# A kernel of cross attention and a two-layer perceptron with its order table, PSUM banks and SBUF rooms laid out anew

## The chip, the cores and the metric

The kernel runs on one core of a Trainium2 chip. The metric is device time in microseconds (us) of one execution. The engines are PE (matrix multiplication, with PEld for its weight loads), DVE (vector), ACT (scalar), POOL (GpSimd) and SP (which here issues transfers). Each works through its own queue in order; semaphores join them.

## The reference

For each of 8 batches and 8 heads, 512 tokens of 64 values and 32 states of 64 values attend to each other in both directions. The result, 544 rows of 512 values per batch, then goes through two layers with a leaky rectifier (alpha per column) between them.

```python
scores = scale * np.matmul(x, state.transpose(0, 1, 3, 2))
a = np.exp(scores - scores.max(-1, keepdims=True))
a /= a.sum(-1, keepdims=True) + 1e-09
xread = np.matmul(a, state)
scores2 = scale * np.matmul(state, x.transpose(0, 1, 3, 2))
...
sread = np.matmul(a2, x)
attn_out = np.concatenate([xread, sread], axis=2)
...
h = x @ w_in
g = np.maximum(h, 0.0) + alpha * np.minimum(h, 0.0)
return (g @ w_out).astype(np.float32)
```

## The kernel before

The work goes by batch. For the tokens of a batch, the states are first multiplied by w_in (m, step `m`, eviction `mo`), and the attention weights of the tokens (aT) then multiply m, so that h comes out at once, without xread. Sixteen tiles h of 128 columns of w_in by 512 tokens are made per batch (step `F`, L568). ACT makes neg = relu(-h) (step `N`, L621), DVE makes g = neg * (1 - alpha) + h (step `G`, L624). The state rows of all batches are gathered in XS and go through the layers as a ninth batch (L577, and steps of number 8).

The second layer of batch 0 is plain: 4 x 16 matmuls of 512 columns (step `S`, L638). For the other batches it is done in seven products of halves instead of eight: sums and differences of quarters of g (gsum, step `U`, L705) and of w_out (ws, step `W`, L681), products in three accumulators px, py, pv (step `P`, L726), copies of intermediate px (kept, step `K`, L742), and output quarters (oq, step `Q`, L759), stored by SP.

The weights of a batch come from scores (sc, L316), a transpose of 32x32 blocks on DVE (ts, L348), a maximum (mx, L381), a shift by it (step `ssh`, L386, mostly POOL), an exponential on ACT (L395), a sum and its reciprocal (r, L402 and L403), a normalisation (an, step `snorm`, L406), and a transpose back (aT, L414). Batch 0 is done in two halves j with PE transposes (tsc, L355; aT from at_ps, L370). The states' own reads of the tokens (sread) go through nb (L426), e (L443), a transposing transfer (e2T) and sr_ps (L469). A fill (step `Z`, L230) is a matmul of a constant pattern whose result is not used; `fill(0, 9)` puts nine of them at PE's start.

What stands where in the queues is not computed: the string ORDER lists some 1,100 steps, each a letter code with its batch, tile, engine (a, v, p for ACT, DVE, POOL) and PSUM bank, and the last loop of the function calls them in turn. Each step puts its instructions at the end of its engines' queues. Eight PSUM banks are six of one tag each (k0 to k5) and a pair with the tag `two`; SBUF tiles have tags by kind, with fixed numbers of buffers (three for xg, four for neg, two per g group).

Of the kernel before, what the change touches and what calls it, by code (L numbers as in the profile page):

```python
# [17 lines left out]
stc.0.a stt.0.1 sbd.0.a cx.0.0.v lst xt.0.0.0.2 cx.1.0.v sbd.1.a xt.0.1.0.3 xo.0.0.0.a tsc.0.0.4 xo.0.1.0.v tsc.1.0  # L18
cx.1.1.v Z.5.1 smax.0.0 xt.0.1.1.0 xo.0.1.1.v cx.0.1.a xt.0.0.1.2 ssh.v.0.0 sto.0.a Z.3.1 tsc.1.1.5 xo.0.0.1.a tsc.0.1
m.0.0.1.3 sexp.0.0 mo.0.0.a.1 Z.0.1 smax.0.1 ssh.v.0.1 sexp.0.1 wi.1 str.0.2 wi.2 sro.0.a ssum.0.0 lx.1 snorm.p.0.0  # L20
str.1.4 wi.3 sro.1.a ssum.0.1 oma Z.0.1 snorm.v.0.1 wo.1 Z.3.1 Z.5.1 m.0.1.0.3 mo.0.1.a.0 at.0.5 mo.0.1.a.1 at.1.2
ao.0.v wo.0 ao.1.v mo.0.0.a.0 m.1.0 mo.1.0.v F.0.7.4 N.0.7 G.0.7 F.0.6.0 F.0.2.5 N.0.6 F.0.1.3 G.0.6 N.0.2 m.2.2.2.1
N.0.1 mo.2.2.v.0 G.0.1 m.1.1 mo.1.1.a F.0.5.4 G.0.2 F.0.4.0 N.0.4 Z.2.1 N.0.5 m.0.2 mo.0.2.a F.0.3.2 F.0.0.3 N.0.0
G.0.4 G.0.5 Z.5.1 xt.1.1.1.0 xo.1.1.1.v G.0.0 N.0.3 G.0.3 F.0.8.5 N.0.8 xt.1.0.1.4 xo.1.0.1.a wo.2 lx.2 F.0.9.0 N.0.9
m.0.3 xt.1.1.0.3 G.0.8 xo.1.1.0.v xt.1.0.0.4 xo.1.0.0.v mo.0.3.a mo.2.2.a.1 Z.2.1 m.3.3.2.5 mo.3.3.a.0 sc.1 m.2.0.3.4
mo.2.0.a.0 mo.2.0.a.1 G.0.9 wo.3 mo.3.3.a.1 F.0.11.1 S.0.1.3.0 sb.1 smax.1 ssh.p.1 S.0.2.3.2 m.2.3.3.4 mo.2.3.a.0
N.0.11 W.1.0.p F.0.10.5 S.0.1.2 tm.1 S.0.2.2 G.0.11 N.0.10 G.0.10 F.0.12.3 W.1.1.p mo.2.3.a.1 S.0.1.0 F.0.14.4 N.0.12
G.0.12 nb.1.a sexp.1 F.0.15.1 ssum.1.5 te.1.1 te.1.0 F.0.13.3 N.0.13 tsum.1 S.0.2.1 snorm.v.1 S.0.1.5 S.0.1.4 N.0.15
m.1.3 mo.1.3.a S.0.1.1 wb.1 G.0.15 S.0.2.5 N.0.14 G.0.14 S.0.2.4 m.1.2 mo.1.2.a G.0.13 S.0.2.0 F.1.1.5 N.1.1 F.1.13.1
G.1.1 N.1.13 G.1.13 F.1.7.4 S.0.2.7 N.1.7 G.1.7 F.1.6.3 N.1.6 S.0.1.7 G.1.6 xd.2 F.1.10.5 N.1.10 G.1.10 F.1.12.1  # L30
S.0.2.6 N.1.12 G.1.12 tt.1 F.1.15.4 O.0.2.a N.1.15 G.1.15 F.1.14.3 N.1.14 G.1.14 W.2.0.p W.4.0.p S.0.1.6 O.0.1.a
S.0.3.7.5 m.6.3.2.1 sc.2 sb.2 mo.6.3.a.1 mo.6.3.a.0 S.0.0.7.4 lx.3 F.1.9.0 N.1.9 W.2.1.p S.0.3.6 F.1.0.3 N.1.0 F.1.5.1
N.1.5 tm.2 smax.2 S.0.0.2 G.1.5 W.3.1.p nb.2.a te.2.1 S.0.3.0 G.1.9 F.1.4.2 S.0.0.3 S.0.3.4 N.1.4 G.1.4 S.0.0.5 G.1.0
te.2.0 tt.2 tsum.2 F.1.11.1 N.1.11 G.1.11 W.4.1.p ssh.p.2 sexp.2 m.3.2 F.1.3.0 N.1.3 ssum.2.2 S.0.0.1 xd.3 S.0.3.2
S.0.3.5 mo.3.2.a S.0.0.4 S.0.3.1 S.0.3.3 F.1.8.3 O.0.3.a N.1.8 F.1.2.1 rd.1.5 G.1.3 rdo.1.1.a rdo.1.0.a snorm.v.2
rd.2.0 rdo.2.1.a m.2.1 G.1.8 rdo.2.0.a N.1.2 G.1.2 mo.2.1.a wb.2 P.1.1.0.1.5 S.0.0.0 S.0.0.6 O.0.0.a P.1.2.0.0.2
U.1.1.1.p sc.3 sb.3 P.1.1.1.0 tm.3 P.1.1.1.1 P.1.1.0.0 K.1.1.a F.2.8.0 F.2.0.3 N.2.8 G.2.8 smax.3 F.2.4.1 F.2.6.4
N.2.0 nb.3.a P.1.2.1.0 N.2.4 U.1.3.1.p N.2.6 G.2.6 P.1.2.0.1 U.1.2.1.p P.1.6.1.1 G.2.0 te.3.1 P.1.2.1.1 G.2.4 te.3.0
tt.3 tsum.3 lx.4 F.2.2.0 N.2.2 xd.4 U.1.1.0.p U.1.2.0.p P.1.6.0.0 P.1.6.1.0 P.1.6.0.1 Q.1.0.0 U.1.4.0.p K.1.2.a
ssh.p.3 F.2.12.4 F.2.15.3 N.2.12 G.2.2 F.2.13.1 G.2.12 N.2.15 G.2.15 F.2.11.2 N.2.11 G.2.11 N.2.13 F.2.5.0 N.2.5  # L40
G.2.13 G.2.5 P.1.5.0.1 P.1.5.1.1 P.1.5.1.0 sexp.3 ssum.3.4 P.1.5.0.0 K.1.4.a rd.3.3 rdo.3.0.a rdo.3.1.a m.3.0.2.1
# [769 lines left out]
```

## Time and profile before

| | |
|---|---|
| median of 3 runs | 209.4 us (209.06 to 209.43) |
| span of the profiled execution, first to last instruction | 207.2 us |
| instructions | 5043 |
| PE busy | 198.9 us, 2003 matmuls |
| DVE busy | 182.6 us |
| ACT busy | 148.7 us |
| POOL busy | 144.0 us |
| granted TensorE clock | 1.00 |

The profiled execution has no time of its own beside its span; the runs' median lies 2.2 us above it. Busy time is the time in which an engine has an instruction under way. A row of the timeline gives start, duration, engine, line, operation, out<-in and how many were merged; a row of groups gives busy us, the mean ns of one, and the idle time just before them with what ended it.

### The profile page before, as it was taken

What the parts mean: (1) busy time and instruction counts of PE and PEld (TensorE: products, weight loads), DVE (VectorE), ACT (ScalarE), POOL (GpSimd) and SP (SyncE); (2) the same over time, 40 slices, a digit from 0 to 9 for tenths busy, and PEclk for the clock granted to TensorE, in tenths of its full rate; (3) what the DMA queues carried; (4) which work ended last, traced back from release to release, by engine and by line L of the source; (5) the groups of instructions that cost most, each with busy time, mean ns of one, the idle gap of its engine ahead of it and who ended that gap; (6) DMA issues with size and microseconds to landing.
All of it is one profiled execution on the core that took longest, in us unless ns stands there. A gap on an engine that the chain in (4) does not pass through costs nothing.

```text
span 207.2 us, 5043 instructions
## 1 busy us (share of the span) xinstructions
PE 198.9 (96%) x2003; PEld 131.7 (64%) x2003; DVE 182.6 (88%) x277; ACT 148.7 (72%) x298; POOL 144.0 (70%) x87
## 2 busy tenths in 40 slices
PE   7789989999999999999999999999999999999992
PEld 2443433445666666677677766778767767888881
DVE  0899999999999999999999999998899988577650
ACT  3799998988789969988786899586677575321211
POOL 8173099999999999999897999949900697210100
PEclk9999999999999999999999999999999999999999
DMA  5999999949599999267979702112002021012134
GB/s 178 223 204 204 206 202 184 116 126 198 92 155 166 175 221 179 38 79 135 252 97 131 214 17 51 55 54 103 0 0 99 6 101 54 0 51 74 48 136 152
DMA packets 45943, 24.74 MB, mean 119 GB/s; under 512 B 24288, under 2 KB 45408, under 8 KB 45920
## 3 DMA queue, kind: packets, MB, share of 16 engines
q1 hardware_dynamic: 32960, 15.74, 31.2%
q0 software_dynamic: 12688, 8.62, 29.2%
q8 instruction: 15, 0.25, 0.5%
q10 hardware_dynamic: 272, 0.07, 0.1%
q14 instruction: 8, 0.07, 0.1%
HBM read 18.36 MB, written 8.91 MB: 132 GB/s over the span
## 4 chain that ended last, share of the span: by engine, by line
PE 81%; DVE 14%; issue 1%; DMA 1%; ACT 1%; POOL 0%; DVEq 0%; POOLq 0%; ACTq 0%
PE px L726 23%; PE h L568 23%; PE pv L726 12%; DVE g L624 7%; PE py L726 6%; PE o L638 6%; PE h L577 3%; PE m_ps L519 3%; PE fill L230 2%; DVE mx L381 1%; PE sr_ps L469 1%; DVE r L402 1%; DMA out_dram<-oq 1%; PE sc L316 1%; DVE ts L386 1%
## 5 line engine op out<-in xcount | busy, mean ns | idle before, releaser
L624 DVE SCALAR_TENSOR_TENSOR g<-neg,oma_sb,h 128x512 f16<-128x512 f32 (+1 forms) x144 | 94.5, 710 | 4.3 <-ACT neg L621 3.5
L621 ACT ACTIVATE neg<-h 128x512 f32<-128x512 f32 (+1 forms) x144 | 76.1, 590 | 14.0 <-PE h L568 8.2
L568 PE MATMUL h<-aT,m 128*128 128x512 f16 x256 | 64.5, 379 | 0.7 <-DVE g L624 0.5
L726 PEld LDWEIGHTS <-gsum 128*128 128x128 f16 x480 | 46.6, 98 | 9.6 <-issue 1.0
L568 PEld LDWEIGHTS <-m 128*128 128x128 f16 x256 | 24.1, 98 | 25.1 <-issue 4.3
L726 PEld LDWEIGHTS <-g 128*128 128x128 f16 x360 | 34.9, 98 | 7.3 <-issue 0.9
L705 POOL TENSOR_TENSOR gsum<-g 128x1024 f16<-128x1024 f16 (+1 forms) x14 | 28.7, 2060 | 14.4 <-PE pv L726 14.3
L705 POOL TENSOR_TENSOR gsum<-g,g 128x1024 f16<-128x1024 f16 x11 | 23.4, 2129 | 13.2 <-DVE g L624 13.1
L726 PE MATMUL px<-ws,gsum 128*128 128x256 f16 x240 | 29.8, 273 | 0.0
L742 ACT COPY kept<-px 128x512 f32<-128x512 f32 (+1 forms) x21 | 12.2, 582 | 23.8 <-PE px L726 22.8
L705 POOL TENSOR_TENSOR gsum<-gsum,g 128x1024 f16<-128x1024 f16 x11 | 23.4, 2126 | 3.4 <-DVE gsum L705 2.7
L705 POOL TENSOR_TENSOR gsum<-g,gsum 128x1024 f16<-128x1024 f16 x11 | 23.4, 2131 | 0.3
L545 ACT CAST m<-m_ps 128x512 f16<-128x512 f32 x36 | 19.9, 622 | 2.8 <-PE m_ps L519 2.7
L386 POOL TENSOR_TENSOR ts<-ts,mx 128x1024 f32<-128x1024 f32 x7 | 13.4, 1916 | 9.3 <-DVE mx L381 8.8
L638 PE MATMUL o<-w_out_sb,g 128*128 128x512 f16 x64 | 16.5, 379 | 0.0
L759 DVE TENSOR_TENSOR oq<-pv,kept 128x512 f32<-128x512 f32 (+1 forms) x16 | 10.5, 653 | 6.7 <-ACT kept L742 4.4
L726 PE MATMUL px<-w_out_sb,g 128*128 128x256 f16 x120 | 16.1, 273 | 0.0
L726 PE MATMUL px<-w_out_sb,gsum 128*128 128x256 f16 x120 | 16.1, 273 | 0.0
L726 PE MATMUL py<-w_out_sb,g 128*128 128x256 f16 x120 | 16.1, 273 | 0.0
L726 PE MATMUL pv<-ws,gsum 128*128 128x256 f16 x120 | 15.7, 273 | 0.0
L726 PE MATMUL pv<-ws,g 128*128 128x256 f16 x120 | 15.6, 273 | 0.0
L543 ACT CAST m<-m_ps 128x1024 f16<-128x1024 f32 x12 | 12.5, 1042 | 1.7 <-PE m_ps L519 1.6
(81 smaller groups left out, 232.7 us busy)
## 6 DMA issues: line engine op xcount, KB each, us to landing
out_dram<-oq SPq DMA_DIRECT2D x28, 256.0 KB, 2.6
xg<-in_x_dram POOLq DMA_DIRECT2D x8, 512.0 KB, 7.4
w_in_sb<-in_moe_w_in_dram POOLq DMA_DIRECT2D x4, 512.0 KB, 8.7
w_out_sb<-in_moe_w_out_dram POOLq DMA_DIRECT2D x4, 512.0 KB, 12.7
x<-in_x_dram SPq DMA_DIRECT2D x2, 512.0 KB, 4.9
out_dram<-osb SPq DMA_DIRECT2D x4, 256.0 KB, 4.3
out_dram<-oq SPq DMA_DIRECT2D x4, 128.0 KB, 2.1
st<-in_state_dram POOLq DMA_DIRECT2D x1, 224.0 KB, 7.3
```

What stands on the lines that cost most here:

```text
L386: engine(e).tensor_tensor(blocks(cols(live["ts", b], j, S)), blocks(scored(b, j)), over_blocks(cols(live["mx", b], j, S // N)), ALU.subtract,)
L519: nc.tensor.matmul(t[N * k : N * (k + 1), :], st_head(b, h)[64 * r : 64 * r + 64, :], w_in_sb[64 * r : 64 * r + 64, c, 512 * f : 512 * (f ...
L543: copier(e)(m_tile(b, f), t)
L545: copier(e)(m_tile(b, f)[:, g, :], t[g])
L568: nc.tensor.matmul(h.rearrange("p (r j s) -> p r j s", r=2, j=2), ms[b, f][:, g, 128 * j : 128 * (j + 1)], weights(b, g), start=(g == 0), ...
L621: nc.scalar.activation(neg, h, RELU, bias=0.0, scale=-1.0)
L624: nc.vector.scalar_tensor_tensor(g_tile(b, jc), negs.pop((b, jc)), oma_sb[:, jc : jc + 1], hs.pop((b, jc)), ALU.mult, ALU.add,)
L638: nc.tensor.matmul(outs[b, q], g_tile(b, jc)[:, 128 * q : 128 * (q + 1)], w_out_sb[:, jc, :], start=not begun and jc == 2 * jc2, stop=left ...
L705: engine(e).tensor_tensor(t, x(), y(), op)
L726: nc.tensor.matmul(pbanks[b, name][:, i, :], of(b, c)[:, j, 128 * i : 128 * (i + 1)], moving[:, 4 * c + j, :], start=not begun and j == 0, ...
L742: copier(e)(t, pbanks[b, "x"])
L759: nc.vector.tensor_tensor(osb, pbanks[b, name], kept[b, add], ALU.add)
```

## The change

All eight PSUM banks become one tile `banks`, and each step names the bank (or the first of two neighbours) that it uses; m, which used the pair or two banks, always uses two free banks and is evicted in two copies. The SBUF tiles that were in tags by kind come from two pools of equal rooms, small ones of 2 KB and large ones of 4 KB per partition; the number behind an @ in ORDER is the room, and a tile that takes a room waits until the last reader of the one before is done. The sum r of the tokens' weights lies in SBUF where the step says `s`; the normalisations on POOL read it there. The loads are issued in another order. ORDER is another list: the same kinds of steps (the same 2003 matmuls, 19 of them fills, six of which move from between the first steps to PE's start behind the nine), in another sequence, on engines partly changed.

```diff
-stc.0.a stt.0.1 sbd.0.a cx.0.0.v lst xt.0.0.0.2 cx.1.0.v sbd.1.a xt.0.1.0.3 xo.0.0.0.a tsc.0.0.4 xo.0.1.0.v tsc.1.0
-cx.1.1.v Z.5.1 smax.0.0 xt.0.1.1.0 xo.0.1.1.v cx.0.1.a xt.0.0.1.2 ssh.v.0.0 sto.0.a Z.3.1 tsc.1.1.5 xo.0.0.1.a tsc.0.1
...
+Z.1.1 Z.2.1 lst cx.0.0.v Z.3.1 Z.4.1 Z.7.1 Z.0.1 wi.1 stc.0.a cx.1.0.a stt.0.5 sbd.0.v sbd.1.v xt.0.0.0.6 xt.0.1.0.1
+xo.0.1.0.v@3 lx.1@4 xo.0.0.0.a cx.0.1.v tsc.0.0.4 tsc.1.0 smax.0.0 xt.0.0.1.3 cx.1.1.a xt.0.1.1.7 xo.0.1.1.v tsc.1.1.2
...
     att = ctx.enter_context(tc.tile_pool(name="att", bufs=2))
-    moe = ctx.enter_context(tc.tile_pool(name="moe", bufs=2))
+    rooms = ctx.enter_context(tc.tile_pool(name="rooms", bufs=1))
...
+    banks = ps.tile([128, 8, 512], F32, name="banks", bufs=1)
...
     def single(k, name, shape, dtype):
-        return ps.tile(shape, dtype, name=name, tag=f"k{k}", bufs=1)
-
-    def two(name, shape, dtype):
-        return ps.tile(shape, dtype, name=name, tag="two", bufs=1)
+        t = banks[:, k, :]
+        return shaped(t.bitcast(F16) if dtype == F16 else t, shape)
+
+    def two(k, name, shape, dtype):
+        return shaped(banks[:, k : k + 2, :].rearrange("p k c -> p (k c)"), shape)
...
+    place = [None]
+
+    def placed(name, shape, dtype):
+        n = 4 if dtype == F32 else 2
+        for d in shape[1:]:
+            n *= d
+        assert n <= 4096
+        tag = f"{'small' if n <= 2048 else 'large'}{place[0]}"
+        room = [shape[0], (2048 if n <= 2048 else 4096) // (4 if dtype == F32 else 2)]
+        return shaped(rooms.tile(room, dtype, name=name, tag=tag, bufs=1), shape)
...
-        xg = xgs[b] = att.tile([128, H, 2, 2, D], F16, name=f"xg_{b}", tag="xg", bufs=3)
+        xg = xgs[b] = placed(f"xg_{b}", [128, H, 2, 2, D], F16)
...
-        if b:
-            live["r1", b] = single(jk, f"r1_{b}", [128, 2 * S // N], F32)
-        r1 = cols(live["r1", b], j, S // N)
+        if b and jk != "s":
+            live["r1", b] = single(jk, f"r1p_{b}", [128, 2 * S // N], F32)
+        r1 = cols(soft_tile(b, "r1"), j, S // N)
...
-    def state_w_in(b, f, k0=None, k1=None):
-        if k0 is None:
-            live["mp", b, f] = two(f"m_ps{b}_{f}", [128, 2, 512], F32)
...
+    def state_w_in(b, f, k0, k1):
+        live["mp", b, f] = k0, k1
+        for g, k in enumerate((k0, k1)):
+            m_matmuls(single(k, f"m_ps{b}_{f}_{g}", [128, 512], F32), b, f, g)
+
+    def state_w_in_out(b, f, e, g):
+        copier(e)(m_tile(b, f)[:, g, :], banks[:, live["mp", b, f][g], :])
...
     for token in (globals().get("TOKENS") or ORDER).split():
+        token, _, where = token.partition("@")
+        place[0] = where
         name, *args = token.split(".")
```

ORDER's other lines are all replaced too. Its effect is shown at three places; names carry buffer numbers of the build.

The first is DVE's start, up to the second shift of batch 0. Before:

```order
L175 CAST xg_first<-x_0_70 128x4x128 x2
L306 COPY xT_first<-xT_psfirst_0_125 128x4x128
L175 CAST xg_first<-x_1_72 128x4x128
L381 TENSOR_REDUCE mx_146<-tsc_132 128x16
L306 COPY xT_first<-xT_psfirst_1_151 128x4x128
L386 TENSOR_TENSOR ts_145<-tsc_132,mx_146 128x512
L381 TENSOR_REDUCE mx_146<-tsc_167 128x16
L386 TENSOR_TENSOR ts_145<-tsc_167,mx_146 128x512
```

And in the change (`banks` is any PSUM bank; L302 copies the states into st_pairs, L215 casts x, L346 copies transposed x):

```order
L215 CAST xg_first<-x_0_71 128x4x128
L302 COPY st_pairs<-banks 64x8x32 x2
L346 COPY xT_first<-banks 128x4x128
L215 CAST xg_first<-x_1_73 128x4x128
L421 TENSOR_REDUCE mx_148<-banks 128x16
L346 COPY xT_first<-banks 128x4x128
L426 TENSOR_TENSOR ts_170<-banks,mx_148 128x512
L421 TENSOR_REDUCE mx_148<-banks 128x16
L426 TENSOR_TENSOR ts_170<-banks,mx_148 128x512
```

The copies into st_pairs have come to DVE, ahead of its first copy of transposed x; the cast of the first half of x has gone to ACT in part.

The second is ACT, from the first exponential of batch 0 to the first neg. Before:

```order
L395 ACTIVATE ts_145<-ts_145 128x512
L545 CAST m_0_188<-m_ps_0_1_178 128x512
L395 ACTIVATE ts_145<-ts_145 128x512
L281 COPY stT<-st_ps_196 128x128x7
L281 COPY stT<-st_ps_218 128x128x7
L545 CAST m_1_258<-m_ps_1_0_248 128x512
L545 CAST m_1_258<-m_ps_1_1_249 128x512
L545 CAST m_0_188<-m_ps_0_0_177 128x512
L621 ACTIVATE neg_7_289<-h_7_286 128x512
```

And in the change (L435 exponential, L571 eviction of m, L321 states, L411 weights aT, L610 neg):

```order
L435 ACTIVATE ts_170<-ts_170 128x512
L571 CAST m_0_181<-banks 128x512
L435 ACTIVATE ts_170<-ts_170 128x512
L571 CAST m_0_181<-banks 128x512
L321 COPY stT<-banks 128x128x7 x2
L411 COPY aT_233<-banks 128x512
L571 CAST m_1_249<-banks 128x512
L571 CAST m_0_266<-banks 128x512
L610 ACTIVATE neg_3_270<-banks 128x512
```

The first half of aT has come to ACT, behind the two copies of the states, and both halves of m for batch 0 are evicted ahead of it; DVE makes the other half of aT.

The third is POOL in the middle, where batches 3 and 4 are normalised. Before:

```order
L386 TENSOR_TENSOR ts_939<-ts_939,mx_940 128x1024
L158 DMA xg_1159<-in_x_dram 128x8x256
L705 TENSOR_TENSOR gsum_4_1_1179<-g_3_607,gsum_2_1_996 128x1024
L158 DMA xg_1195<-in_x_dram 128x8x256
L705 TENSOR_TENSOR gsum_3_0_1212<-g_0_603 128x1024
L681 TENSOR_TENSOR ws_736<-w_out_sb 128x1024
L705 TENSOR_TENSOR gsum_1_1_1274<-g_1_990,g_3_1061 128x1024
```

And in the change (L426 shift, L446 normalisation, L692 sums of g, L196 load of x):

```order
L426 TENSOR_TENSOR ts_912<-ts_912,mx_941 128x1024
L692 TENSOR_TENSOR gsum_4_1_1016<-g_3_574,gsum_2_1_727 128x1024
L692 TENSOR_TENSOR gsum_4_0_1048<-g_2_723,gsum_2_0_901 128x1024
L692 TENSOR_TENSOR gsum_3_1_1082<-g_1_586 128x1024
L446 TENSOR_TENSOR an_1094<-ts_912,r_3_1012 128x1024
L692 TENSOR_TENSOR gsum_3_0_1101<-g_0_927 128x1024
L692 TENSOR_TENSOR gsum_1_1_1103<-g_1_957,g_3_950 128x1024
```

The normalisation an of the batch stands on POOL, between sums of g; before it was DVE's, in this stretch `L406 TENSOR_TENSOR an_941<-ts_939,r_3_1094 128x1024`.

300 lines of the change are left out of this document (136 added, 164 removed).

## The prediction

> **What bounds the kernel now.** I read the page's busy shares and its chain first, then a table by stage.
>
> ```profile
> PE 198.9 (96%) x2003; PEld 131.7 (64%) x2003; DVE 182.6 (88%) x277; ACT 148.7 (72%) x298; POOL 144.0 (70%) x87
> ...
> PE 81%; DVE 14%; issue 1%; DMA 1%; ACT 1%; POOL 0%; DVEq 0%; POOLq 0%; ACTq 0%
> ```
>
> PE is busy for 198.9 of 207.2 us and carries 81% of the chain that ended last. An average over stages hides where the other 8.3 us lie, so here are five stages (us of the stage, then busy us and instructions of PE, PEld, DVE, ACT, POOL):
>
> ```profile
> 0.00:5.20 5.20, 3.75 (x9) 1.19 (x9) 0.39 (x3) 1.58 (x2) 4.49 (x12) 1.00 0.55 179
> 5.20:15.50 10.30, 8.24 (x109) 4.41 (x109) 9.39 (x20) 8.47 (x16) 4.24 (x6) 1.00 1.25 213
> 15.50:40.00 24.50, 23.44 (x208) 9.64 (x206) 24.39 (x37) 23.63 (x44) 15.64 (x11) 1.00 1.22 183
> 40.00:140.00 100.00, 99.92 (x1187) 66.04 (x1164) 98.47 (x139) 84.74 (x178) 93.49 (x49) 1.00 0.69 129
> 140.00:201.00 61.00, 61.00 (x499) 48.53 (x497) 48.52 (x81) 29.32 (x59) 26.14 (x13) 1.00 0.16 57
> ```
>
> From 40 to 201 us PE is without a matmul for 0.08 us. Nothing that the change does to other engines there can make it faster; it can only keep PE as full. Up to 40 us DVE and ACT are the full ones: from 15.5 to 40 DVE rests 0.11 us and ACT 0.87, and PE 1.06. From 40 to 140 DVE still rests only 1.5 of 100 us. So the time is: the moment at which the DVE and ACT work of batch 0 gets going, plus a PE stream that must not break. The end is short:
>
> ```profile
> 202.27 1.04 PE L726 MATMUL px<-w_out_sb,gsum 128*128 128x256 f16 x8
> ...
> 203.40 0.37 ACT L757 COPY oq<-px 128x256 f32<-128x256 f32 x1 [1.22 <-PE px L726]
> ```
>
> The last useful matmul ends at 203.3, and 3.9 us of eviction and store follow. The change ends in the same way (a quarter of the state rows, from DVE instead of ACT), so I leave this tail as it is. The median of the three runs is 209.4, the span of the profiled execution 207.2; the 2.2 us around it are carried over.
>
> **The start, step by step.** These rows of the timeline (start, us, engine, operation) are the path to the first h and the first g:
>
> ```profile
> 1.45 4.02 PE L230 MATMUL fill<-pattern 128*128 128x512 f16 x9 [1.45 <-POOL pattern L210]
> ...
> 4.88 0.30 ACT L248 CAST st<-st 128x128 f16<-128x128 f32 x1 [2.35 <-DMA st<-in_state_dram]
> ...
> 5.17 1.16 DVE L175 CAST xg_first<-x 128x512 f16<-128x512 f32 x2 [3.99 <-DMA x<-in_x_dram]
> ...
> 5.40 0.42 PE L242 MATMUL st_ps<-ident,st 128*64 128x128 f16 x4
> ...
> 5.87 0.74 ACT L262 COPY st_pairs<-st_ps 64x256 f16<-64x256 f16 x2 [0.69 <-PE st_ps L242]
> ...
> 6.05 0.73 PE L300 MATMUL xT_psfirst<-ident,xg_first 128*128 128x128 f16 x8 [0.23 <-DVE xg_first L175]
> ...
> 6.81 0.42 DVE L306 COPY xT_first<-xT_psfirst 128x512 f16<-128x512 f16 x1 [0.49 <-PE xT_psfirst L300]
> ...
> 7.28 0.41 PE L355 MATMUL tsc<-st_pairs,xT_first 128*128 128x64 f16 x8 [0.50 <-ACT xT_first L306]
> ...
> 7.72 0.69 DVE L381 TENSOR_REDUCE mx<-tsc 128x16 f32<-128x512 f32 x1
> ...
> 10.08 0.69 DVE L386 TENSOR_TENSOR ts<-tsc,mx 128x512 f32<-128x512 f32 x1
> ...
> 11.04 0.82 PE L230 MATMUL fill<-pattern 128*128 128x512 f16 x3
> 11.34 2.07 ACT L281 COPY stT<-st_ps 128x896 f16<-128x896 f16 x2
> ...
> 12.80 0.68 DVE L406 TENSOR_TENSOR an<-ts,r 128x512 f16<-128x512 f32 x1
> ...
> 14.21 1.91 PE L568 MATMUL h<-aT,m 128*128 128x512 f16 x8
> ...
> 14.86 2.07 ACT L621 ACTIVATE neg<-h 128x512 f32<-128x512 f32 x4
> ...
> 15.49 1.41 DVE L624 SCALAR_TENSOR_TENSOR g<-neg,oma_sb,h 128x512 f16<-128x512 f32 x2
> ```
>
> Before, the nine fills end about when the first states are cast (5.18), and PE goes on at 5.40. In the change six of the ten later fills stand behind those nine, ahead of everything else on PE. Nine take 4.02 us, so 0.43 each; the three at 11.04 take 0.82 with their latency, so nearer 0.22. The transposes at 6.05 (eight in 0.73) already run fast. Between six at 0.22 (1.3 us) and six at 0.43 (2.6 us) I take two slow and four fast, 1.7: PE reaches the transposed states at 6.9, **1.5 us later**, though their data is there. PE is in order, so the transposes of x wait too.
>
> From there I follow the new rows with the old durations. The two st_pairs copies go from ACT (0.37 each) to DVE (not seen there; at most the 0.42 of its copy of twice the size, at least half of it; I take 0.3): 7.2 to 7.8. They stand ahead of DVE's xT copy (to 8.2), and that ahead of its cast of the second half of x (to 8.75). ACT's own xT copy (0.6) ends at 8.0, so the first tsc runs at 8.1 instead of 7.28; its second eight follow DVE's copy, and the first mx starts at 8.8 instead of 7.72. Back to back on DVE come mx, the other xT copy and the first shift (to 10.55, some 0.06 under the rows' sum, since neighbours overlap); then DVE waits for the second tsc, which needs that copy (10.7); the second mx and shift end at 12.05 instead of 10.77. Two sums with their reciprocals (0.9 each with the wait for the second exponential, which ends on ACT at 12.7) and the an row bring the last an piece to 14.35 instead of 13.48. ACT now has, after that exponential, one m cast (0.6), the two stT copies (2.07, to 15.4) and only then the first half of aT (0.6, to 16.0), which was DVE's. The first h starts at **16.05 instead of 14.21 (+1.85)**. Two m casts stand on ACT between it and the first neg, so neg comes at 17.1 instead of 14.86 and g at **17.75 instead of 15.49 (+2.25)**. The loads are not late for this: the order of the first three (w_in 0, states, w_in 1) is kept, and the next batch's x comes earlier. That they contend is bounded below by nothing and above by one load's turn, 512 KB at the 213 GB/s of that stage, 2.5 us:
>
> ```profile
> w_in_sb<-in_moe_w_in_dram POOLq DMA_DIRECT2D x4, 512.0 KB, 8.7
> ```
>
> I take nothing, since PE asks for these weights about 1.5 us later than before, and so later than their place in the queue asks for.
>
> **The steady part.** PE has the same 2003 matmuls, so PE's stream is priced at no change. On the other engines these rows price what moves (busy us, mean ns of one):
>
> ```profile
> L624 DVE SCALAR_TENSOR_TENSOR g<-neg,oma_sb,h 128x512 f16<-128x512 f32 x128 | 88.5, 740 | 4.1 <-ACT neg L621 3.5
> ...
> L406 DVE TENSOR_TENSOR an<-ts,r 128x1024 f16<-128x1024 f32 x7 | 8.5, 1214 | 0.0
> ...
> L386 POOL TENSOR_TENSOR ts<-ts,mx 128x1024 f32<-128x1024 f32 x7 | 13.4, 1916 | 9.3 <-DVE mx L381 8.8 <-ACT e L443 0.4
> ...
> L705 POOL TENSOR_TENSOR gsum<-g,g 128x1024 f16<-128x1024 f16 x11 | 23.4, 2129 | 13.2 <-DVE g L624 13.1
> ...
> L545 ACT CAST m<-m_ps 128x512 f16<-128x512 f32 x36 | 19.9, 622 | 2.8 <-PE m_ps L519 2.7
> ...
> L543 ACT CAST m<-m_ps 128x1024 f16<-128x1024 f32 x12 | 12.5, 1042 | 1.7 <-PE m_ps L519 1.6
> ...
> L757 ACT COPY oq<-px 128x512 f32<-128x512 f32 x7 | 4.1, 589 | 3.7 <-PE px L726 3.7
> ```
>
> DVE loses five of its seven 1024-wide normalisations: 5 x 1.214 = 6.1 us less. It gains two output copies, the st_pairs copies, one more m cast's worth and some scalings, some 1.9 us at the rates of its neighbours; net **-4.2**. POOL gains those five at 1.92 to 2.13 (say 2.05), **+10.2**, and goes from 144 to about 154 of 207: still free, but each such row now stands in POOL's queue with gsum rows behind it, and the batch's aT waits 0.8 us longer for it than on DVE. ACT gets 24 casts of 622 ns for 12 of 1042 (+2.4) and gives back some copies; net **+0.7**, no relief.
>
> Now the lateness meets the slack. PE, 1.85 late at its first h, can win back what it idled up to 40 us, at most 1.06; the change has a next m and second-layer products ready early, and I take 0.6. DVE starts its g work 2.25 late. To 40 us it is fed by ACT, which is full there and has no less to do; followed row by row, DVE rests another 2.4 us in 17.75 to 40. So DVE is 4.65 late against 4.2 us less work by 140 us: 0.45 short, and the chain shows that DVE's lateness is paid there:
>
> ```profile
> 125.72 1.12 DVE mx L381
> 126.84 3.35 DVE g L624 x6
> ...
> 130.70 0.74 DVE g L624
> ```
>
> Bounds of this term: nothing (the 4.2 come early enough) and 2.25 (they come after PE has needed them); nearest to the row-by-row count, 0.5. **Sum:** 209.4 + 1.85 - 0.6 + 0.5 = 211.2 us.
>
> All eight PSUM banks may now hold anything, instead of six single ones and a pair. That could let PE run further ahead, which from 40 us on has 0.08 us to give. In SBUF a room is taken again when its last reader is done; the transposed x of batches 2, 3 and 0 share one room, so each load waits for the scores of the one before. SP queues nothing else of the path behind these; I take nothing.
>
> **Rivals.** *A, faster.* The first h is not bound by the fills (its data comes later in most executions than in the profiled one), and PE, fed earlier with the second layer, wins the 1.06 us of 15.5 to 40 and about 1 us of the 2.06 between 5.2 and 15.5. For it: DVE's relief. Against it: the cast rows at 4.88 and 5.17, ahead of the fills' end. Time 209.4 - 2.0 = 207.4. *B, much slower.* Every step has a new place, and ACT, DVE and POOL wait for each other in order. ACT, 2.25 late and with 0.7 more work, had only 0.87 us of rest to 40; where neg is late, g is late, its bank is held, and the h queued behind on PE waits. It decides from one such break per batch on: eight at 0.5 give 4 us more than the first h's 1.85 alone would, 213.5 to 215. Against it: 15.3 us of rest on ACT from 40 to 140. *C, no change.* PE's reordered work takes up the whole 1.85: 209.4. *D, the clock.* The six fills taken from the stretch from 7 to 23 us filled pauses of PE; with those open PE may drop to the slow rate of the first fills, and h at 0.43 instead of 0.22 (eight in 1.91 with their latency) for some 4 us costs 2 us more: 213.2. The granted clock reads 1.00 throughout before. The Trainium skill (TensorE: Matmul & The Clock Gate, "What's actually happening") says that the array falls to half rate after an idle window of some 3.4 us and is released after as long a busy one, at a moment that shifts from run to run; the rows at 1.45 and 6.05 agree with the release, and no run yet shows the fall.
>
> **How the numbers follow.** Forecast 0.44 (own range 210.2 to 212.6), A 0.25, B 0.16, C 0.10, D 0.05. Against 0.2% (0.4 us), about what this measurement can tell from no change: faster is A, 0.25; within is C and a little of the forecast's edge, 0.11; slower 0.64. The range reaches A's 207.4 and B's upper half, 214.5.
>
> **What would show it.** Right: st_ps starts near 6.9 and the first g near 17.75; fills sum to the same; POOL near 154 busy, DVE near 178; PE idle some 1 to 2 us more before 16 and nearly none from 40 to 200. Wrong: first g at or before 15.5 (A); PE idle spread over 40 to 140 behind g or gsum (B); a granted clock under 1 around 10 to 20 us (D). A first g as late as forecast with an unchanged end would refute the terms behind it.

## The result, and the profile after

The change is slower by far more than forecast: 231.26 us (median of 4 runs, 230.37 to 231.48) against 209.32 for the kernel before, measured with it, a ratio of 1.1043 with a 95% interval of 1.1022 to 1.1064. The forecast was 211.2 with a range to 214.5. The direction was right, and the size was wrong by 20 us.

The page of the change, busy time by engine and the granted clock in 40 slices:

```profile
PE 205.9 (90%) x2003; PEld 133.8 (58%) x2003; DVE 188.8 (82%) x276; ACT 147.8 (64%) x305; POOL 155.8 (68%) x94
...
PEclk9999999859999999999999999999999999979999
```

The span is 229.5, 22.3 us more than before. PE's idle time makes 15.3 of it (23.6 for 8.3) and PE's own work 7.0 (205.9 for 198.9, the same 2003 matmuls): the clock row has two dips where it had none. By stage (us, then busy us of PE, PEld, DVE, ACT, POOL, and the granted clock):

```profile
15.50:40.00 24.50, 24.18 (x195) 9.94 (x196) 24.14 (x36) 24.00 (x50) 18.74 (x13) 1.00 1.31 200
40.00:60.00 20.00, 15.04 (x97) 6.38 (x96) 12.63 (x16) 11.32 (x24) 12.20 (x7) 0.83 0.87 155
60.00:80.00 20.00, 17.88 (x212) 11.91 (x210) 18.46 (x27) 16.60 (x37) 18.46 (x11) 1.00 0.76 123
...
180.00:200.00 20.00, 16.68 (x140) 13.39 (x137) 18.38 (x25) 6.67 (x14) 13.42 (x8) 1.00 0.00 1
```

From 15.5 to 40 us PE is even fuller than before (24.18 of 24.50, was 23.44). Apart from the late start, the loss begins at 40. PE's waits of the change, by what ended them (total us, times, longest):

```profile
PE banks L355 <- DMA xT<-xg: 5.0, 1, 5.0
PE banks L507 <- DMA e2T<-e: 2.6, 1, 2.6
PE banks L590 <- DVE g L613: 2.5, 3, 1.3
PE banks L713 <- DVE gsum L692: 2.0, 1, 2.0
```

The two longest are waits for transposing transfers, of x (batch 2, at 40.4) and of e (batch 3, at 77.9). The first transfer was issued at 31.5, as before, but lay 13.8 us before it landed; before it took 5.9. Ahead of it POOL had issued loads of x for batches 2, 3, 6, 4 and 0, and in this stretch the kernel before had issued only one. Three of POOL's five issues (the first, the fourth and the last), and then the transfer's duration on SP (ns) and its landing (us), in the change and before:

```profile
15.10 0.90 POOL L196 DMA_DIRECT2D xg<-in_x_dram  x1
...
21.50 0.87 POOL L196 DMA_DIRECT2D xg<-in_x_dram  x1 [1.63 <-DMA w_out_sb<-in_moe_w_out_dram]
...
24.46 0.91 POOL L196 DMA_DIRECT2D xg<-in_x_dram  x1
```
```profile
L331 SPq DMA_TRANSPOSE xT<-xg x1: 5490/5490/5490, 31.5 to 31.5; - x1
DMA to landing us min/median/max: 13.8/13.8/13.8
```
```profile
L291 SPq DMA_TRANSPOSE xT<-xg x1: 3060/3060/3060, 31.4 to 31.4; - x1
DMA to landing us min/median/max: 5.9/5.9/5.9
```

And the clock behind that wait, by short stretches (the number before the last two is the granted clock):

```profile
44.00:46.00 2.00, 0.64 (x24) 0.32 (x24) 0.00 (x0) 0.00 (x0) 0.74 (x1) 0.62 1.25 274
46.00:48.00 2.00, 2.00 (x12) 0.59 (x5) 1.94 (x2) 1.17 (x3) 0.00 (x0) 0.50 1.29 216
48.00:52.00 4.00, 4.00 (x12) 1.50 (x11) 3.48 (x5) 2.95 (x9) 1.66 (x1) 0.59 0.53 83
```

The clock is halved for 1.5 + 2.0 + 3.3 = 6.8 us. The first 0.9 of them still lie within the wait, which ends at 45.4, so the half clock costs PE some 3.0 us on top of the 5.0. That is the stage from 40 to 52.

The third place is the end. From 160 to 206 us sums of g stand on DVE and POOL at the same time, and DVE's are long. DVE, and the POOL rows beside them:

```profile
180.48 2.53 DVE L692 TENSOR_TENSOR gsum<-g,g 128x1024 f16<-128x1024 f16 x1
...
191.69 0.68 DVE L692 TENSOR_TENSOR gsum<-gsum,g 128x1024 f16<-128x1024 f16 x1
...
201.82 2.32 DVE L692 TENSOR_TENSOR gsum<-g,gsum 128x512 f16<-128x512 f16 x1 [1.05 <-POOL gsum L692]
```
```profile
180.35 2.12 POOL L692 TENSOR_TENSOR gsum<-gsum,g 128x1024 f16<-128x1024 f16 x1
...
201.75 3.41 POOL L692 TENSOR_TENSOR gsum<-g,gsum 128x1024 f16<-128x1024 f16 x2
```

At 191.69, where DVE was first, such a sum takes 0.68, and POOL's beside it 3.1 instead of 2.1; the others shown began just after one of POOL's and end after it. In the kernel before no sum of DVE ran beside one of POOL's, and none took over 0.7. One group of them, before and in the change (busy us, mean ns):

```profile
L705 DVE TENSOR_TENSOR gsum<-g,gsum 128x1024 f16<-128x1024 f16 x3 | 2.1, 692 | 0.4 <-PE px L726 0.2
```
```profile
L692 DVE TENSOR_TENSOR gsum<-g 128x1024 f16<-128x1024 f16 x5 | 7.0, 1407 | 0.0
```

Added up over all groups, 15 sums take DVE 18.6 us in the change, and 17 took 9.8 before. That is most of why DVE's busy time, forecast at 178, is 188.8.

### The profile page after: what moved, and what is told of

Its sections match the earlier page's. It is cut to its first block, busy times and chain, and to the rows that moved or that the text cites. A ratio compares the mean times of both kernels' runs of the same rounds, so it can differ in the third digit from the quotient of the medians.

```text
span 229.5 us, 5038 instructions
## 1 busy us (share of the span) xinstructions
PE 205.9 (90%) x2003; PEld 133.8 (58%) x2003; DVE 188.8 (82%) x276; ACT 147.8 (64%) x305; POOL 155.8 (68%) x94
## 5 line engine op out<-in xcount | busy, mean ns | idle before, releaser
L613 DVE SCALAR_TENSOR_TENSOR g<-neg,oma_sb,banks 128x512 f16<-128x512 f32 (+1 forms) x144 | 93.9, 706 | 3.7 <-ACT neg L610 3.3
L610 ACT ACTIVATE neg<-banks 128x512 f32<-128x512 f32 (+1 forms) x144 | 77.0, 596 | 22.0 <-PE banks L590 14.4
L590 PE MATMUL banks<-aT,m 128*128 128x512 f16 x256 | 69.4, 387 | 3.0 <-DVE g L613 2.5
L713 PEld LDWEIGHTS <-gsum 128*128 128x128 f16 x480 | 47.3, 99 | 15.5 <-DVE gsum L692 2.3
L713 PE MATMUL banks<-ws,gsum 128*128 128x256 f16 x360 | 48.3, 278 | 0.0
L571 ACT CAST m<-banks 128x512 f16<-128x512 f32 x60 | 34.3, 626 | 12.4 <-PE banks L555 11.6
L692 POOL TENSOR_TENSOR gsum<-g,g 128x1024 f16<-128x1024 f16 (+1 forms) x14 | 28.9, 2066 | 10.4 <-DVE g L613 7.0
L713 PE MATMUL banks<-w_out_sb,g 128*128 128x256 f16 x240 | 32.1, 274 | 0.0
L692 POOL TENSOR_TENSOR gsum<-gsum,g 128x1024 f16<-128x1024 f16 (+1 forms) x13 | 27.1, 2087 | 5.4 <-DVE gsum L692 4.7
L692 POOL TENSOR_TENSOR gsum<-g 128x1024 f16<-128x1024 f16 (+1 forms) x10 | 20.7, 2079 | 8.7 <-DVE g L613 8.7
L692 POOL TENSOR_TENSOR gsum<-g,gsum 128x1024 f16<-128x1024 f16 (+1 forms) x12 | 24.6, 2065 | 0.1
L426 POOL TENSOR_TENSOR ts<-ts,mx 128x1024 f32<-128x1024 f32 x7 | 13.4, 1911 | 14.4 <-DVE mx L421 14.2
L627 PE MATMUL banks<-w_out_sb,g 128*128 128x512 f16 x64 | 17.0, 394 | 0.0
L446 POOL TENSOR_TENSOR an<-ts,r 128x1024 f16<-128x1024 f32 (+1 forms) x6 | 10.6, 1771 | 6.6 <-DVE r L443 5.3
```

The source lines that it names most:

```text
L426: engine(e).tensor_tensor(blocks(cols(soft_tile(b, "ts"), j, S)), blocks(scored(b, j)), over_blocks(cols(live["mx", b], j, S // N)), ALU.s ...
L446: engine(e).tensor_tensor(blocks(cols(soft_tile(b, "an"), j, S)), blocks(cols(live["ts", b], j, S)), over_blocks(cols(live["r1", b], j, S ...
L571: copier(e)(m_tile(b, f)[:, g, :], banks[:, live["mp", b, f][g], :])
L590: nc.tensor.matmul(h.rearrange("p (r j s) -> p r j s", r=2, j=2), ms[b, f][:, g, 128 * j : 128 * (j + 1)], weights(b, g), start=(g == 0), ...
L610: nc.scalar.activation(neg, h, RELU, bias=0.0, scale=-1.0)
L613: nc.vector.scalar_tensor_tensor(g_tile(b, jc), negs.pop((b, jc)), oma_sb[:, jc : jc + 1], hs.pop((b, jc)), ALU.mult, ALU.add,)
```

## The experiments

"Late" and "forward" below mean places in the list ORDER; every kernel is the change or the kernel before with only what its diff shows.

**The transfer and its echo.** The theory: four loads queued ahead hold the transfer, and the half clock is PE's own pause coming back.

```diff
-lx.3@12 lx.6@13 lx.4@14 W.1.0.p@15 lx.0@16
+W.1.0.p@15   (lx.3 behind W.4.0, lx.4 and lx.0 behind U.1.2.1, lx.6 ahead of lx.5)
```

> The change with four loads of x issued later (batch 3 behind POOL's sums of w_out, batches 4 and 0 behind the first sums of g, batch 6 just ahead of batch 5); nothing else moves. Theory T (the transposing transfer of x of batch 2 queues behind these loads): it takes 5 to 7 us instead of 13.8, PE's wait of 4.96 us at 40.4 goes, and so does the granted clock of 0.5 that follows it (6.83 us, worth about 3.4 us); the time falls by 7.5 to 8.5 us, to 222.8 to 223.8. Rival R1 (that transfer is late for another reason, its data or its queue): the wait stays, time 231.3 within 1. Rival R2 (the wait goes, but PE's work ran ahead of DVE and only pays elsewhere): the wait goes, the time falls by less than 4 us.

> The change with only two of these loads issued later (batches 4 and 0); batches 3 and 6 stay where they are. Theory T with 2.5 us for each load of 512 KB: the transposing transfer takes 13.8 - 5.0 = 8.8 us and lands at 40.3, within 0.3 us of the moment at which PE asks; no fall of the granted clock; time as with all four late, within 1.5 us. If one of the loads left is enough to hold it (R1), it takes over 12 us.

Measured: 228.9 (ratio 1.094, 1.0921 to 1.096) and, one run, 229.9. The transfer of batch 2 took 5.0 us with four late and 10.8 with two, after 13.8 with none; the two landings:

```profile
DMA to landing us min/median/max: 5.0/5.0/5.0
```
```profile
DMA to landing us min/median/max: 10.8/10.8/10.8
```

Each load ahead of it costs 1.5 to 2.9 us. The wait at 40 is gone in the first (2.5 left in the second). So the cause of that wait is shown, but the time fell by 2.4 us, not 8: my new places put four loads (issued from 52.8 to 59.8) just ahead of the next transfers, and the wait moved there:

```profile
PE banks L507 <- DMA e2T<-e: 5.8, 1, 5.8
```

The echo was parted from the wait by giving PE fills to do while it waits:

```diff
-sc.2.1
+Z.1.22 sc.2.1
```

> The change with 22 more fills (4.75 us at 0.216) on PE in front of the scores of batch 2, so that PE runs on while it waits for the transfer; the transfer itself is as late as before. This parts the wait from its echo. If the pause of PE is what makes the granted clock fall, the clock stays at 1.00 from 44 to 51 us and the 6.83 us at 0.5 cost 3.4 us less: time 227.9 (227 to 229). If the fall has another cause, or the slow stretch is hidden behind DVE, the time stays at 231.3 within 0.5.

Measured: 228.17 (1.0905, 1.0881 to 1.093), 3.1 us less than the change, with the transfer as late as ever:

```profile
40.48 4.91 PE L270 MATMUL banks<-pattern 128*128 128x512 f16 x22
45.33 0.41 PE L355 MATMUL banks<-xT,stT 64*32 64x256 f16 x16
```
```profile
46.00:48.00 2.00, 2.00 (x10) 0.88 (x9) 2.00 (x2) 1.97 (x5) 0.00 (x0) 1.00 1.27 223
```

Work that computes nothing makes the kernel faster: in the profiled execution the clock stays at 1.00, and a 5.0-us wait of PE was worth 8. The Trainium skill (TensorE: Matmul & The Clock Gate, "What's actually happening") says that an idle window of some 3.4 us drops the array to half rate; here a wait of 5.0 did, and without it the clock did not fall.

**SP's queue, and where the loads go.** Next e of batch 3 was transposed ahead of x of batches 0 and 4 instead of behind them, first with the loads as above, then with the loads spread.

```diff
-xd.0@18 xd.4@7 tt.3@41
+tt.3@41 xd.0@18 xd.4@7
```

> The change with the four loads late, and besides the transposing transfer of e of batch 3 issued ahead of the two transposing transfers of x of batches 0 and 4 on SP instead of behind them; nothing else. With the loads late alone PE waited 5.8 us at 70 us for that e2T, and the clock fell to 0.5 for 3.75 us after it. Theory (SP's queue: e was ready some 10 us before SP reached its transfer, because the two transfers ahead wait for rooms and data): the wait at 70 goes, and its clock fall with it; 5.8 + 1.9 = 7.7 us, of which some returns as DVE's limit: time 221.5 (220 to 223.5). Rival (batch 3's e, or DVE, is what is late): the wait stays and the time is 228.9 within 1. Rival (the transfers of x of 0 and 4 are now late): a wait of the same size stands at the scores of batch 4.

Measured: 229.47 (1.0952, 1.0916 to 1.0988), no gain. The third possibility came true: e2T's wait fell to 1.1 us and the scores of batch 4 waited as long as e2T had, since the loads still lay ahead:

```profile
PE banks L355 <- DMA xT<-xg: 5.8, 1, 5.8
```

So the order on SP mattered less than the loads. With them spread (lx.3 behind W.4.0, lx.0 behind W.1.1, lx.4 behind U.1.1.1, lx.6 and lx.5 behind U.1.3.1), and e still ahead on SP:

> The change with the five loads of x of batches 3, 0, 4, 6 and 5 spread out (issued near 36, 38, 50 and, two of them, after 66 us), so that at most one stands in the queue when a transposing transfer is issued, and e of batch 3 transposed ahead of x of 0 and 4. In the two kernels before it, four loads stood in the queue at 53 to 62 us and the transfers of 61 to 73 us took 12 us. Theory Q (a transposing transfer waits for the loads queued ahead, 2.5 us each): every transfer lands within 7 us, PE's waits at 40 and from 70 to 79 us go, the clock stays at 1.00 to 180 us; time 231.3 - 8.5 (40 to 52 us) less what DVE's own limit takes back: 222 (219 to 225). Rival (the waits move on whatever is done to the loads): a wait of 4 us or more at a new place before 120 us, time above 226.

Measured: 222.84 (1.0657, 1.0599 to 1.0715), 8.4 us less than the change, for the loads and SP's order together. In its profiled execution every transfer of x lands within 5.8 us, none of PE's five longest waits is for a transfer, and the clock falls only at 191.9. This is the largest part of the 22 us that one experiment moves. What is left of PE's waits is mostly DVE's, with the two of 2.5 and 2.0 us that the change has too.

**DVE beside POOL.** Loops on data in SBUF, alone and together (start, us, engine; L58 and L61 are sums of g, L64 is g with one input from PSUM, L67 scales two values). The first block has rows of DVE, the second the rows of POOL beside two of them, and the last two give the shortest, the median and the longest of one instruction (ns):

> No part of the reference is computed: DVE and POOL run loops alone and at the same time on SBUF, in six stretches. Theory: a sum of g on DVE (two inputs from SBUF) takes 0.68 us alone and 1.4 to 1.7 beside a sum of g on POOL, and POOL's 2.13 grows too; a g (one input from PSUM), measured at 740 ns beside POOL and alone, does not change. Rival: DVE's sums were long in the change because their inputs or their place differ (or because of DMA traffic); then they take 0.68 here in both stretches. Open: the scaling of two values (0.48 alone, 1.1 to 1.3 at one place of the change), the 32x32 transposes and copies from PSUM, which follow either the one or the other.

```profile
21.54 18.93 DVE L58 TENSOR_TENSOR do<-ga,gb 128x1024 f16<-128x1024 f16 x12
...
41.09 2.71 DVE L64 SCALAR_TENSOR_TENSOR go<-neg,al,h 128x512 f16<-128x512 f32 x4
...
44.44 10.61 DVE L64 SCALAR_TENSOR_TENSOR go<-neg,al,h 128x512 f16<-128x512 f32 x16
...
59.64 15.38 DVE L67 TENSOR_SCALAR nb<-nb 128x2 f32<-128x2 f32 x20
```
```profile
22.35 15.16 POOL L61 TENSOR_TENSOR po<-pa,pb 128x1024 f16<-128x1024 f16 x6
...
44.86 12.51 POOL L61 TENSOR_TENSOR po<-pa,pb 128x1024 f16<-128x1024 f16 x6
```
```profile
L58 DVE TENSOR_TENSOR do<-ga,gb x24: 678/682/2598, 8.9 to 39.8; 128x1024 f16<-128x1024 f16 x24
```
```profile
L67 DVE TENSOR_SCALAR nb<-nb x24: 159/170/2040, 58.1 to 74.8; 128x2 f32<-128x2 f32 x24
```

Alone a sum takes 0.68. While POOL's six sums run, DVE's take up to 2.60, and POOL's grow from 2.09 to 2.53 (12.51 and 15.16 for six): they take turns, whole instruction by whole instruction. I had expected 1.4 to 1.7. The text calls this the lock. The scaling of two numbers goes from 0.17 to 2.04. A g is not touched (some 0.67 each in both stretches), nor is a copy from PSUM, nor a 32x32 transpose, although that one has both of its operands in SBUF. The Trainium skill (GPSIMD Engine Reference, "Key points") says that GpSimd shares its SBUF interfaces with VectorE, with contention for DVE instructions with two SBUF inputs or in a two-port mode; the loops agree, and show besides that here it is a turn of up to one whole POOL instruction.

In the change, the last eleven of POOL's sums were given to DVE, alone and with the loads changed:

```diff
-U.6.1.1.p U.6.2.1.p U.6.2.0.p U.7.1.1.p U.7.1.0.p U.8.1.1.p U.8.1.0.p U.8.3.1.p U.8.2.0.p U.7.4.1.p U.8.4.1.p
+U.6.1.1.v U.6.2.1.v U.6.2.0.v U.7.1.1.v U.7.1.0.v U.8.1.1.v U.8.1.0.v U.8.3.1.v U.8.2.0.v U.7.4.1.v U.8.4.1.v
```

> The change with the last eleven sums of g that were POOL's (of batches 6, 7 and the states) on DVE, at the same places of the list; nothing else. Theory L (an instruction of DVE that reads and writes SBUF only waits out the POOL instruction of its kind that is under way, and the other way round, as in the two loops): the sums on DVE take 0.68 (1024 wide) and 0.41 (512 wide) each, DVE gets 6 x 0.68 + 5 x 0.41 = 6.1 us of work and gives back 7.7 us of lock, and PE's waits from 180 to 206 (6.3 us, and the clock's fall at 201.5) shrink to below 3: time 227 (225.5 to 229). Rival (the sums were long for their own inputs' sake): they stay at 1.0 to 1.6, DVE's work grows by 9 to 15 us there and the time rises by 3 or more.

> Loads late, the reads first, and the last eleven sums on DVE. If the parts are independent, their gains add: 231.3 less the gain of loads and reads (some 10) less that of the sums (some 4) = 217.5 (215 to 220). If they share one limit (DVE), the sum falls short of that by 2 us or more.

> Loads spread and the last eleven sums of POOL on DVE. With the change alone this gave nothing (231.45 for 231.3): the lock's 7.4 us went, 6.1 us of work came, and DVE was full from 160 to 190 us. If DVE reaches that stretch earlier now, the sums find free time on it: 1.5 to 3 us lower than with the loads spread alone. If DVE is still full there: within 1 us.

Measured: 231.45 (1.1041, 1.1013 to 1.107) on the change, 229.73 (1.0963, 1.0938 to 1.0987) with the loads late, and a ratio of 1.0663 (1.0607 to 1.0719, 223.3 us) with the loads spread: nothing in all three. The lock did go (nearly all sums take 0.68), but now PE waits for sums on DVE that stand there behind g's and other sums. In the first of the three:

```profile
180.00:200.00 20.00, 15.80 (x121) 12.01 (x119) 15.12 (x28) 5.80 (x13) 0.00 (x0) 0.91 0.00 1
```
```profile
PE banks L713 <- DVE gsum L692: 4.5, 3, 2.9
```

PE is 15.80 busy in that stage for 16.68 in the change. The theory had counted DVE's time and not its order. So what the lock itself costs the change in time is not shown.

Then the sums were parted in time: four early ones that DVE made from 157 to 181 to POOL, six late ones of POOL to DVE, without and with the scalings nb of batches 5 and 7 on ACT.

> Loads spread (222.8), and besides the last sums of g so that DVE and POOL make them at different times: four sums that DVE made from 157 to 181 us go to POOL, which rests there, and six of POOL's last (the five of the states and one of batch 7) go to DVE, which rests there. With the loads spread DVE was full from 160 to 180 us (20.00 of 20), three of its sums there took 2.17 to 2.53 instead of 0.68, and PE waited 7.3 us from 157 to 196 with the clock's fall behind them. Theory (DVE is the limit of that stretch, and the lock is a good part of its work): DVE's sums take 0.68 and 0.41 nearly everywhere, DVE is freed of 7.1 us from 157 to 181, PE's waits of 157 to 196 fall from 7.3 to under 2: time 217 (215.5 to 219). Rival (the limit is not DVE's time but the order in which g, neg and banks wait for each other): within 1.5 us of 222.8.

> The same, and the scaling of two values for batches 5 and 7 on ACT instead of DVE. On DVE it took 1.09 us at 95.9 us, beside a sum of POOL; ACT's kind takes 0.22 at the rows of other batches. PE waited 1.42 us there for the scores' banks. Theory (the lock, on a small instruction that others wait for): 0.8 to 1 us of that wait goes, time 0.5 to 1 us lower than without. Rival: nothing, since ACT is late for the exponential in any case.

Measured: ratios of 1.0856 (1.0779 to 1.0932, 227.2 us) and 1.0694 (1.0638 to 1.075, 223.9 us). DVE's busy time fell to 181.9 and 179.8 from 189.2, and PE now waited for POOL, whose queue had two sums that nobody waited for yet ahead of those that PE needed (a row of the second kernel):

```profile
179.90 1.03 PE L713 MATMUL banks<-ws,gsum 128*128 128x256 f16 x4 [5.75 <-POOL gsum L692]
```

The difference between the two is not the scalings' alone: up to 150 us the first is the kernel with the loads spread, yet in its profiled execution PE waited 3.5 us at 57 for a transfer of x (batch 3), and there it did not. That transfer was issued 4.0 us ahead of the load of batch 4 with the loads spread, and it landed in 5.8 us; in the five other traces with the loads in the same places it was 1.9 to 2.4 us ahead, landed in 7.8 to 9.9, and PE waited 1.5 to 4.2. So a load issued behind a transfer seems to hold it too, and the profile of the loads spread is a lucky one in that. At 99 us, where the scaling had stood, the wait for the scores' banks is 0.34 for 1.42 before, as expected.

Last, all of it together: loads of batches 4 and 0 behind U.1.2.1, nb on ACT, the four sums that can wait on POOL, behind the urgent ones, all others of batches 6, 7 and the states on DVE.

> All that was found, put into the change: loads spread (those of batches 4 and 0 behind the second sums of g, so that none is issued just after a transposing transfer of x), e of batch 3 first, the two small scalings on ACT, and the sums of g of batches 6, 7 and the states by their use: the four that nobody waits for on POOL (behind the urgent ones), all others on DVE. Theory: PE's waits behind POOL's sums of the kernel with the sums apart (5.75 and 1.04 us from 174 to 182) go, DVE's sums take 0.68; 222.8 less 3 to 5 us: 218.5 (216.5 to 221). Rival (DVE is full there whatever is done): 222 to 224.

Measured: 220.5 (1.0521, 1.0473 to 1.057), the best of the kernels built on the change, 10.8 us below it, and still 11 above the kernel before. PE's longest wait is again at the first sums of batch 6:

```profile
PE banks L713 <- DVE gsum L692: 3.7, 2, 2.4
```

From 156.6 to 175.6 DVE makes 28 g's and only one sum ahead of them. Of the 11 us, PE's waits from 170 to 187 with their half clock are some 7.5; whether another order could take them away was not tried.

**The normalisations.** The five that the change gave to POOL were put back on DVE, with the loads spread:

> Loads spread, and the five normalisations that the change gave to POOL back on DVE; the sums as in the change. The prediction's term (DVE is the limit from 40 us on, and these five are 6.1 us of it): 4 to 6 us slower than with the loads spread, 227 to 229. Rival (the normalisations on POOL lengthen the way of each batch's weights by 0.7 us and lock DVE's small instructions, and that weighs as much): within 1.5 us of 222.8.

Measured: 232.65 (1.1102, 1.1018 to 1.1186), 9.8 us slower than with the loads spread. Two groups of the same instruction on DVE tell why it is more than the 6.1 of work (busy us, mean ns):

```profile
L446 DVE TENSOR_TENSOR an<-ts,r 128x1024 f16<-128x1024 f32 x5 | 11.6, 2312 | 0.0
...
L446 DVE TENSOR_TENSOR an<-ts,banks 128x1024 f16<-128x1024 f32 x2 | 2.4, 1214 | 0.0
```

With the sum r in PSUM, as in the kernel before for batches 1 to 7, it takes 1.21 beside a busy POOL; with r in SBUF, as the change has it for batches 3 to 7, it is locked out and takes 2.31. The transfer of x of batch 3 was late in this trace too, and PE waited 2.2 us for it, so not all of the 9.8 is the normalisations'.

**Each part alone, in the kernel before.** The kernels above scatter by 1 to 2 us and the kernel before, measured beside those below, by 0.4, so three parts of the change were put into it one by one: the six fills to PE's start, fourteen sums of batches 6, 7 and the states on the engines that the change has them on, five normalisations on POOL with r in SBUF.

> The kernel before, with only this part of the change: six fills (three of 7 to 10 us, three of 17 to 23 us) moved to PE's start behind the nine. The prediction's step: the transposed states 1.5 us later, st_ps at 6.9 instead of 5.40, and at the end 1.5 to 1.9 us, 211. Rival (what the change showed: by 40 us PE had done as much as before, since three fills fewer stand after 17 us): first g later by about 1 to 1.5 us, time within 0.5 us of 209.4.

> The kernel before, with fourteen sums of g of batches 6, 7 and the states on the engine on which the change has them (six from POOL to DVE, eight from DVE to POOL), each at its old place. The lock alone, in a kernel whose PE is full: DVE's sums beside POOL's take 1.4 to 2.6 us instead of 0.68, and those on POOL 2.13 instead of 0.68. DVE was busy 12.7 of 20 us from 180 to 200 before, so if the lock costs only DVE's free time the time stays within 0.5 us of 209.4; if PE waits for the sums, as in the change, it is 2 to 5 us slower.

> The kernel before, with the five normalisations of batches 3 to 7 on POOL instead of DVE, their sums r in SBUF. The prediction's step for DVE (6.1 us less work from 40 to 140 us, where it rests 1.5): faster if DVE is the limit there, but PE is without a matmul for only 0.08 us from 40 to 201, so at most the noise: 209.4 within 0.5. Rival (each stands in POOL's queue behind sums, POOL was busy 19.4 to 19.8 of 20 us from 40 to 100): aT is late and PE waits, 0.5 to 1 us a batch, 2 to 5 us slower.

Measured: **210.9** (1.0085, 1.0054 to 1.0116), **214.32** (1.0263, 1.0211 to 1.0315) and a ratio of **1.0278** (1.0246 to 1.031, 215.1 us). No trace of the third is read here, so its mechanism is only argued (aT late behind POOL's queue). The medians mix two things. Of the eight runs of the first, four took 210.1 to 210.4 us at a granted clock of 1.000, and three 212.1 at 0.992; 0.8% of 210 us is 1.7, so these three lost about what 3.4 us at half clock would cost. The second and third have runs at 0.988 and 0.989 too, 0.6 to 2.5 us above their others. Where the clock fell in them is not known, since none of them was traced.

The first, in an execution that ends 0.8 us later than the profiled one before:

```profile
1.45 5.10 PE L230 MATMUL fill<-pattern 128*128 128x512 f16 x15 [1.45 <-POOL pattern L210]
...
15.05 1.92 PE L568 MATMUL h<-aT,m 128*128 128x512 f16 x8
```

Here h starts 0.84 late and the span is 0.8 longer (208.0 for 207.2): what the start loses is paid in full, and the rest of the 1.6 us by which the median is higher comes from the runs at the lower clock. The second, whose span is 4.1 longer: PE waits 2.7 us at 201 for a sum on DVE that waits for POOL's, the last of four in a row:

```profile
197.59 2.12 POOL L705 TENSOR_TENSOR gsum<-g,gsum 128x1024 f16<-128x1024 f16 x1
```
```profile
199.74 1.35 DVE L705 TENSOR_TENSOR gsum<-gsum,g 128x512 f16<-128x512 f16 x1 [3.59 <-POOL gsum L705]
```
```profile
201.15 1.05 PE L726 MATMUL px<-ws,gsum 128*128 128x256 f16 x8 [2.71 <-DVE gsum L705]
```

So POOL's slower sums in the chain cost more there than the lock (1.35 for 0.42 is the lock's).

In the change the fills were also taken back, with the loads late and with the loads spread:

> The kernel with loads late and the reads first, and besides the six fills that the change put at PE's start taken back to between the first steps (three between 7 and 10 us, three after 17). The prediction's term (they make the first h 1.85 us and the first g 2.25 us late, 1.75 of it paid at the end): first g about 1.5 to 2 us earlier, and the time 1.5 to 2 us below that kernel. Rival (by 40 us PE has in the change done as much as before, so the lateness is already won back): first g earlier, the time within 0.5 us of it.

> The same with the six fills taken back from PE's start to between the first steps. The prediction's term: 1.75 us lower than the kernel with the loads spread. Rival (already won back by 40 us): within 0.5 us of it.

Measured: 228.55 (1.0917, 1.0867 to 1.0966) against 229.47 without, and 224.93 (1.0704, 1.0634 to 1.0774) against 222.84: the intervals overlap, and the difference goes once each way; nothing can be told. One reason may be in the start of both, where PE still ran slowly behind the nine fills, and eight transposes took 1.03 us or more instead of the change's 0.62 (the granted clock reads 1.00 there in every trace; the slow rate shows in the durations alone). The row of the second:

```profile
6.08 1.03 PE L340 MATMUL banks<-ident,xg_first 128*128 128x128 f16 x8 [0.20 <-DVE xg_first L215]
```

## Why the prediction was wrong, step by step

- **The start, right.** These rows of the change stand against the forecast:

```profile
1.45 6.10 PE L270 MATMUL banks<-pattern 128*128 128x512 f16 x15 [1.45 <-POOL pattern L250]
7.48 0.30 PE L282 MATMUL banks<-ident,st 128*64 128x128 f16 x4
...
15.89 1.46 PE L590 MATMUL banks<-aT,m 128*128 128x512 f16 x6
```
```profile
17.35 2.06 DVE L613 SCALAR_TENSOR_TENSOR g<-neg,oma_sb,banks 128x512 f16<-128x512 f32 x3
```

  The states came at 7.48 (forecast 6.9), h at 15.89 (16.05) and g at 17.35 (17.75). The six fills cost 6.10 - 4.02 = 2.1 for 1.7, and the steps behind them less than priced: the 0.6 by which the states were later than forecast had shrunk to 0.2 at the end of the second exponential (12.9 for 12.7). That h is met within 0.2 is partly luck, also because the same fifteen fills took 4.72 and 6.35 us in other traces. What PE wins back to 40 us was 0.74 (24.18 for 23.44), forecast 0.6. The six fills alone, in the kernel before, cost 0.8 us by the trace and 1.6 by the median (1.1 to 2.4 by the interval); the forecast's 1.85 - 0.6 + 0.5 = 1.75 was for these and other moved steps, so the nearness proves little.
- **The 0.5 for DVE, without ground.** It came from DVE resting another 2.4 us from 17.75 to 40; there DVE was busy for 22.03 of 22.25.
- **"I take nothing" for the loads, wrong; the largest error.** The step asked only whether the loaded data comes in time for its own users, and bounded the contention by one load's turn, 2.5 us. It did not ask what else uses the transfers at that moment. The transposing transfer of batch 2 was held for 7.9 us more than before, PE waited 5.0, and the half clock took some 3.0 more. Spreading the loads, with e ahead on SP, gave 8.4 us back.
- **"SP queues nothing else of the path behind these", wrong.** The transfer of e of batch 3 stood behind those of x of batches 0 and 4, and PE waited 2.6. Cured with the loads late it gave nothing (229.47 for 228.9), so its share can't be told from the loads'.
- **"From 40 us on PE can only keep full", right as a sentence and wrong in its use.** It is why every wait after 40 is paid, and I listed no term there but DVE's 0.45.
- **The durations carried over for DVE, wrong.** The rows of before were true for DVE's sums beside an idle POOL, and for normalisations with r in PSUM. DVE's busy time came out at 188.8, forecast 178; POOL's, 155.8 for 154, was right. That POOL would take five normalisations and other sums for nothing was the mistake: the step saw each batch's aT wait 0.8 us longer and gave that no term. In the kernel before the normalisations alone cost 5.8 and the sums 5.0 us. The three parts and the loads make 1.6 + 5.0 + 5.8 + 8.4 = 20.8 of the 21.9 us; they were measured in different kernels, so that they add up so closely is no proof that they are independent. What the lock alone adds to the time stays open, since taking it away with the sums on DVE gained nothing, and no run changes the banks or the rooms apart from the order. In the change itself the normalisations are better on POOL than on DVE with r in SBUF (by up to 9.8 us).
- **The rivals.** B had the kind right (PE idle in breaks after 40) and gave it 0.16, but its mechanism, neg late on ACT, did not decide: ACT is busy 147.8 us, less than before. D had the clock's fall right and its place wrong: in the trace of the change it came after waits at 40 and 198, not at the start, where the fills taken away left no mark; in the kernel before with only the fills moved, three of eight runs had a lower clock, and where it fell in them is open. A and C fell with the first h.

## What to carry to other kernels

Before pricing a load that moves at nothing, list every transfer that is issued while it is queued, and who waits for those. A duration read from a row holds only for the neighbours it had there: for DVE sums and scalings whose operands are all in SBUF, ask what POOL runs at that moment. Where the matrix engine is full, a wait can cost more than its length (here 5.0 us cost 8), and fills in front of the waiting matmul can buy part of it back (here 3.1).

## What the runs showed of the hardware that I had not expected

- In the loops DVE and POOL take turns by whole instructions on sums and scalings that lie in SBUF alone: 0.68 becomes 2.60 and 0.17 becomes 2.04. A g or a copy that reads PSUM keeps its duration, and so does a 32x32 transpose in SBUF. Moving a small operand from PSUM to SBUF put an instruction under this lock (1.21 to 2.31).
- A transposing transfer of 512 KB took 5.0, 10.8 and 13.8 us with none, two and four of the moved loads queued ahead, and another one 5.8 to 9.9 us as a load was issued 4.0 to 1.9 us behind it.
- The wait that is followed by the half clock has no fixed length here: 5.0 us at 40 and 2.0 at 198.5 were, 2.6 at 77.9 was not; with two loads late, 2.5 at 40 was. The same fifteen fills took 6.10 us in the change and 4.72 with the loads spread, as the fast rate came later or sooner. The Trainium skill (TensorE: Matmul & The Clock Gate, "What's actually happening") explains such shifts by a free-running window; the runs agree and can't show the window itself.
